# The opening of a mixed attention and feed-forward kernel: value row 0 loaded whole ahead of x, x turned by whole transposes between the first value products

## The chip, the cores and the metric

The kernel runs on one core of a Trainium2 chip. Its time is the device time of one execution in microseconds. The core has a matrix engine (PE, with its weight loads shown apart as PEld), a vector engine (DVE), a scalar engine (ACT), a general engine (POOL) and a sync engine (SP), which here only issues transfers. Each takes its instructions in the order in which they were written and waits on semaphores. 16 DMA engines carry out the transfers that SP and ACT issue.

## The reference

```python
x = A_x                                          # [1, 2048, 640] bf16
g = sigmoid((x * gate_w).sum(-1, keepdims=True))
q, k, v = split(x @ wqkv)                        # 32 heads of 20
phi(u) = concat(softmax(u @ w_phi), softmax(-(u @ w_phi)))   # per head
a = (phi(q) @ (phi(k).T @ v)) / (phi(q) @ sum(phi(k)) + 1e-6) @ wo
b = (gelu(x @ w_gate) * (x @ w_up)) @ w_down     # 640 -> 1728 -> 640
out = g * a + (1 - g) * b
```

All inputs and the output are bf16. The matrix products need x with its 640 features on the partitions, so x has to be turned; the kernel holds it as `xT`, five blocks of 128 features by 2048 tokens.

## The kernel before, in words

Tokens are worked in 16 tiles of 128. The kernel runs in stages: the values, keys and queries of all tiles with the state of the linear attention, then the feed-forward part with the attention's numerators between, then the down projections with the output. The order of all instructions is written out by hand; a small helper, `_Sched`, records for each tile or PSUM bank (a key such as `("ps", 2)`) who wrote and read it last, and adds the waits that follow from that.

The change lies in the first 12 us, in `loads` and in the head of `attention_state`. Only tiles 0 to 3 are concerned. Tiles 4 and up are turned by transposing transfers (`xturn`, L236).

*Transfers.* SP issues, in order: x tiles 0 and 1 (`xload("sp", 0)`), x tiles 2 and 3, the value columns of `wqkv` row block by row block (L249 to L251; row 0 in two pieces, columns 0 to 255 and 256 to 639, keys `("wv", 0)` and `"wv0"`), three chunks of `w_up`, then the transposing transfers of x tiles 4 and 5 and of the key columns `wkT`, and more. ACT issues two small ones: `w_phi` (L276; it waits for POOL's second mask) and the gate vector into `gz` (L279).

*Turning x.* PE first runs dummy products on constants (L675): six of 512 columns, three of 128. `x_transpose(t, ek)` turns a tile by ten transposes of 64 tokens by 128 features, against a 64x64 identity, in two row groups that go to two PSUM banks each, banks (0,1), (4,5), (2,3), (6,7) for tiles 0, 1, 2, 3. One copy per tile takes them to `xT`: DVE for tiles 0 and 2, ACT for tile 1, and half each for tile 3. Six more dummies stand between tiles 1 and 2.

*Values.* `v_step(t, kt)` multiplies feature block `kt` of tile `t` with row block `kt` of the value weights: 480 columns into bank `t`, 160 into bank 4 or 5. A tile needs five such steps. Block 0 is done in two parts per tile (0: the first 256 columns, 1: the others), tiles 0 and 1 first; then blocks 1, 2 and 3 for all tiles.

*Behind it.* `blockdiag` (DVE, L361) spreads `w_phi` with the masks into block-diagonal matrices, in five products. `gate_column(6)` transposes `gz` on PE into bank 6 (L370), and DVE copies it into the weights (L372). Then come block 4 of the four tiles with the copies of the values (ACT and DVE by turns, L493 and L495), three up projections of the feed-forward part (`up_ahead`, L464, into banks 7, 6 and 4), the values of tiles 4 and 5, and the folding of `w_phi` into the key weights (L404), which needs the block-diagonal matrices and `wkT`.

Of the kernel before, what the change touches and what calls it, by code (L numbers as in the profile page):

```python
# [3 lines left out]
P = 128  # L4
BF16 = mybir.dt.bfloat16
F32 = mybir.dt.float32
AF = mybir.ActivationFunctionType
# [100 lines left out]
class _Kernel:  # L108
    S, D, H, DH, F = 2048, 640, 32, 20, 1728
    KD = D // P  # L110
# [111 lines left out]
    def loads(self):  # L222
        sc, nc = self.sc, self.nc
        D, KD, DH, P_ = self.D, self.KD, self.DH, P
        w3 = self.wqkv.rearrange("(kt p) n -> p kt n", p=P)
# [3 lines left out]
        def xload(q, j):  # L229
            sc.dma(q, lambda e: e.dma_start(self.xtok[:, j:j + 2, :], x4[:, j:j + 2, :]),  # L230
                   writes=[("xtok", j), ("xtok", j + 1)])
# [4 lines left out]
        def xturn(t, n):  # L236
# [5 lines left out]
              writes=["gtmp"])  # L242
# [1 line left out]
        sc.op("pool", lambda e: e.affine_select(self.ident[:, :], self.ident[:, :], pattern=[[-1, P]],  # L244
                                                compare_op=ALU.not_equal, fill=1.0, base=0, channel_multiplier=1),
              writes=["ident"])
        xload("sp", 0)
        xload("sp", 2)
        for kt in range(KD):  # L249
            for a, z, key in ((0, self.VA, ("wv", 0)), (self.VA, D, "wv0")) if kt == 0 else ((0, D, ("wv", kt)),):  # L250
                sc.dma("sp", lambda e: e.dma_start(self.w3[:, kt, a:z], w3[:, kt, 2 * D + a:2 * D + z]), writes=[key])  # L251
        u3 = self.wu.rearrange("(kt p) n -> p kt n", p=P)
        a, z = self.UP[0] * P, 7 * P
        sc.dma("sp", lambda e: e.dma_start(self.wu_sb[:, :, a:z], u3[:, :, a:z]), writes=["wue"])
# [4 lines left out]
               writes=["wul"])  # L259
# [5 lines left out]
        for i in range(KD):  # L265
            n = self.HHI[i] - self.HLO[i] + 1
# [6 lines left out]
            pool(lambda e, m=m, n=n, base=base: e.affine_select(  # L273
                m, m, pattern=[[DH, n]], compare_op=ALU.is_ge, fill=0.0, base=DH - 1 - base, channel_multiplier=-1),
                [("mask", i)])
        sc.dma("act", lambda e: e.dma_start(  # L276
            self.wphi_sb[:, :, :], self.wphi.rearrange("h d f -> (h d) f").rearrange("(i p) f -> p i f", p=P)),
            reads=[("mask", 1)], writes=["wphi"])
        sc.dma("act", lambda e: e.dma_start(self.gz[0:KD, :], self.gw.rearrange("(k p) -> k p", p=P)), writes=["gz"])  # L279
        for r in (0, 1):  # L280
            m = self.hmask[:, r, :]
            pool(lambda e, m=m: e.memset(m, 1.0), [("hmask", r)])
# [47 lines left out]
            self.load(self.wd_sb[64 * r:64 * r + 64, 13, :], self.wd[13 * P:self.F, :], ("wd13", r))  # L330
        self.load(self.wo_sb[:, :, :], self.wo.rearrange("(kt p) n -> p kt n", p=P), "wo")

    def x_transpose(self, t, ek):

        sc = self.sc
        b, w = (0, 4, 2, 6)[t], self.D // 2
        bks = (b, b + 1)
        pv = self.bank(b, 1024).bitcast(BF16).rearrange("p (r c) -> p r c", r=2)[:, :, 0:w]
        for c in range(self.KD):
            for r in (0, 1):  # L340
                a = 64 * r
                sc.op("pe", lambda e: e.transpose(
                    pv[:, r, c * 64:(c + 1) * 64], self.xtok[a:a + 64, t, c * P:(c + 1) * P],
                    self.ident[a:a + 64, a:a + 64]),
                    reads=[("xtok", t), "ident"], writes=[("ps", bks[r])], signal=(c == self.KD - 1))
        out = self.xT[:, :, t * P:(t + 1) * P].rearrange("p c (r t) -> p c r t", t=64)
        src = pv.rearrange("p r (c t) -> p c r t", t=64)
        rd = [("ps", b) for b in bks]
        if ek == "ad":
            sc.op("act", lambda e: e.activation(out[:, :, 0, :], src[:, :, 0, :], AF.Copy), reads=rd[:1], writes=[("xh", t)])  # L350
            sc.op("dve", lambda e: e.tensor_copy(out[:, :, 1, :], src[:, :, 1, :]), reads=rd[1:], writes=[("xT", t)])
        elif ek == "a":
            sc.op("act", lambda e: e.activation(out, src, AF.Copy), reads=rd, writes=[("xT", t)])
        else:
            sc.op("dve", lambda e: e.tensor_copy(out, src), reads=rd, writes=[("xT", t)])

    def blockdiag(self):
        DH = self.DH
# [111 lines left out]
            self.mm(bank, bcol, n, self.xT[:, kt, t * P:(t + 1) * P], self.w3[:, kt, c0:c0 + n], kt == 0,  # L470
                    kt == self.KD - 1, [("xT", t)] + [(k, kt) if k != "wgate" else k for k in keys])

    def v_step(self, t, kt, part=None):
        sc = self.sc
        tail = (480, 160, 4 + t // 3, 160 * (t % 3))
        parts = ([(0, self.VA, t, 0)], [(self.VA, 480 - self.VA, t, self.VA), tail], [(0, 480, t, 0), tail])
        for c0, n, bk, col in parts[2 if part is None else part]:
            sc.op("pe", lambda e, c0=c0, n=n, bk=bk, col=col: e.matmul(  # L478
                self.bank(bk)[:, col:col + n], self.xT[:, kt, t * P:(t + 1) * P], self.w3[:, kt, c0:c0 + n],
                start=(kt == 0 and col == 0), stop=(kt == self.KD - 1), skip_group_check=True),  # L480
                reads=[("xT", t), ("xh", t), "wv0" if part == 1 else ("wv", kt)], writes=[("ps", bk)],
                signal=(kt == self.KD - 1))

    def v_first_evac(self, ts, ek, tail):
        sv, nt = ts[0], len(ts)
# [184 lines left out]
    def attention_state(self):  # L670
        NT = self.NT
        sc = self.sc
        ones = self.nc.const_aps.tensor(1.0, [P, 512], BF16)
        for n in (512, 512, 512, 512, 512, 512, 128, 128, 128):
            sc.op("pe", lambda e: e.matmul(self.bank(0, n), ones[:, 0:P], ones[:, 0:n], start=True, stop=True),  # L675
                  writes=[("ps", 0)])
        vs, ve, xt = self.v_step, self.v_first_evac, self.x_transpose
        xt(0, "d")
        xt(1, "a")
        for i in range(3):  # L680
            for a, b in ((0, 2), (64, 3)):
                sc.op("pe", lambda e: e.matmul(self.bank(b, P), ones[a:a + 64, 0:P], ones[a:a + 64, 0:P], start=True,
                                               stop=True), writes=[("ps", b)])
        xt(2, "d")
        xt(3, "ad")
        for t, part in ((0, 0), (1, 0), (0, 1), (1, 1), (2, 0), (2, 1), (3, 0), (3, 1)):
            vs(t, 0, part)
        for kt in range(1, 4):
            for t in range(4):
                vs(t, kt)  # L690
        self.blockdiag()
        self.gate_column(6)
        for t in range(4):
            vs(t, 4)
            ve([t], "ad"[t % 2], False)
            if t == 2:
                ve([0, 1, 2], "a", True)
        ve([3], "d", True)
        v, k, q = self.v_tile, self.k_tile, self.q_tile
        self.up_ahead(0, 7, "d")  # L700
        self.up_ahead(1, 6, "a")
        self.up_ahead(2, 4, "d")
        v(4, 2)
        self.v_split(5, 0)
        m, t, p = "main", "tail", "strip"
        self.fold("k", (3, 4, 6, 5, 7), (0, 1), [(m, 0), (m, 1), (m, 2), (m, 4), (p, 6), (t, 0), (t, 1)])
        v(6, 2)
        v(7, 4)
        k(0, 6)
        self.up_ahead(3, 0, "a")  # L710
        self.up_ahead(4, 2, "a")
        self.k_sums(0)
        self.fold("q", (4, 5, 0, 3, 1), (6, 7), [(m, 0), (m, 1), (p, 4), (m, 2), (m, 4), (p, 0), (t, 0), (t, 1), (p, 5)],
                  2)
        k(1, 2)
        k(2, 4)
        k(3, 0)
        v(8, 2)
        self.strip(1, "a", self.KN)
        self.k_scale(0)  # L720
        for t in range(1, 4):
            self.k_norm(t)
        nk, nv, ng, nq = 4, 9, 0, 0
        self.nq, self.half = 0, 1
        pieces = self.gate_pieces()

        def turn():
            self.half ^= 1
            return (5, 0)[self.half]
        for s in range(NT):  # L730
            r = s % 4
            if r != 1:
                if nk in (4, NT - 1):
                    k(nk, turn())
                else:
                    self.kq_tile(nk, turn())
                self.k_norm(nk)
                nk += 1
            if s and r != 0:
                self.gram(ng)  # L740
                ng += 1
            if s and r in (0, 1):
                v(nv, turn())
                nv += 1
            if s == NT - 1 or r == 1 or s == 0:
                q((0, 4, 1, 2, 3, NT - 1)[nq], turn())
                nq += 1
            if s:
                pieces.pop(0)()
        for p in pieces:  # L750
            p()
        self.down_weights()
# [286 lines left out]
```

## Time and profile before

| | us |
|---|---|
| time, median of three executions | 283.66 (283.25 to 283.87) |
| the profiled execution: span from its first to its last instruction | 282.4 |
| the profiled execution's own time, by the profile | its span; nothing is shown of what lies around it |
| PE busy, of that span | 278.6 |
| PE at work without a break from | 6.19 |
| first up projection starts on PE | 11.53 |
| granted PE clock, mean over the span | 1.00 |

Lines of the timeline have start, duration, engine, line and what is written from what, with the idle time before it and what ended that in brackets. Lines of groups have the busy time of all and the mean of one. Those of transfers have the size and the time from issue to landing. Times are in us from the start of the span, means in ns.

### The profile page before, as it was taken

Reading aid. Unit: us, or ns where it says so; the run is one execution under the profiler, and the core shown is the slowest. Engines: PE = TensorE matmul, PEld = TensorE weight load, DVE = VectorE, ACT = ScalarE, POOL = GpSimd, SP = SyncE. Lnnn points to the kernel's source line nnn. Section 1 sums busy time; section 2 is a strip of 40 time slices with the busy share of each in tenths; the row PEclk is TensorE's granted clock in tenths of the full one; section 3 lists DMA queues with packets and bytes.
Section 4 is the critical chain, followed back from the end, with each engine's and each line's share of the span. In section 5 each row is a group of like instructions: output and inputs, shape, how many; then the busy total and the mean of one; then the engine's idle time right before and its main releaser. Section 6 shows DMA issues by size and latency. Waiting matters only on the chain.

```text
span 282.4 us, 6904 instructions
## 1 busy us (share of the span) xinstructions
PE 278.6 (99%) x2926; PEld 168.6 (60%) x2926; DVE 173.2 (61%) x329; ACT 105.9 (38%) x204; POOL 15.1 (5%) x69
## 2 busy tenths in 40 slices
PE   7999999999999999999999999999999999999996
PEld 4566766665665444444444444445777777777786
DVE  1456999999997523694333324235883883883801
ACT  3246978777793332223232232321112112112011
POOL 7511001101000000000000000000000000000000
PEclk9999999999999999999999999999999999999999
DMA  7999169787789910011000000000133132532221
GB/s 213 193 223 190 29 127 172 153 175 149 157 175 274 350 51 0 2 24 23 2 0 0 0 2 0 0 0 2 26 50 98 46 49 78 66 49 73 73 72 49
DMA packets 60378, 24.11 MB, mean 85 GB/s; under 512 B 51002, under 2 KB 59834, under 8 KB 60346
## 3 DMA queue, kind: packets, MB, share of 16 engines
q1 hardware_dynamic: 59680, 23.63, 38.9%
q8 instruction: 23, 0.38, 0.6%
q10 hardware_dynamic: 666, 0.03, 0.2%
q14 instruction: 9, 0.07, 0.1%
HBM read 9.04 MB, written 2.62 MB: 41 GB/s over the span
## 4 chain that ended last, share of the span: by engine, by line
PE 97%; DMA 1%; SPq 0%; ACT 0%; issue 0%
PE ps L464 58%; PE ps L898 29%; PE ps L599 4%; PE ps L817 2%; PE ps L478 2%; PE ps L637 2%; DMA w<-in_A_wqkv_dram 1%; PE ps L404 1%; SPq L230 0%; SPq L251 0%; ACT outsb L911 0%; PE ps L370 0%
## 5 line engine op out<-in xcount | busy, mean ns | idle before, releaser
L464 PE MATMUL ps<-xT,wu_sb 128*128 128x512 bf16 x260 | 64.1, 379 | 0.0
L464 PE MATMUL ps<-xT,wg_sb 128*128 128x512 bf16 x260 | 63.9, 379 | 0.0
L779 ACT ACTIVATE gl<-ps 128x512 bf16<-128x512 f32 x52 | 31.0, 597 | 70.3 <-PE ps L464 70.3
L464 PE MATMUL ps<-w,xT 128*128 128x362 bf16 (+5 forms) x340 | 51.4, 302 | 0.0
L898 PE MATMUL ps<-wd_sb,hT 64*128 64x320 bf16 x648 | 48.4, 296 | 0.0
L781 DVE TENSOR_TENSOR hT<-ps,gl 128x512 bf16<-128x512 f32 x34 | 23.4, 689 | 37.7 <-PE ps L464 37.7
L464 PEld LDWEIGHTS ps<-xT,wu_sb 128*128 128x128 bf16 x260 | 25.4, 98 | 30.3 <-DVE hT L781 0.2
L464 PEld LDWEIGHTS ps<-xT,wg_sb 128*128 128x128 bf16 x260 | 25.1, 98 | 29.8 <-issue 0.2
L911 ACT ACTIVATE outsb<-ps,Gm 128x320 bf16<-128x320 f32 (+2 forms) x31 | 14.5, 515 | 71.8 <-PE ps L898 71.8
L464 PEld LDWEIGHTS ps<-w,xT 128*128 128x128 bf16 x340 | 31.9, 97 | 14.8
L898 PEld LDWEIGHTS ps<-wd_sb,hT 64*128 64x128 bf16 x648 | 30.9, 94 | 12.2 <-issue 0.4
L898 PE MATMUL ps<-wo_sb,goT 64*128 64x320 bf16 (+2 forms) x340 | 26.5, 288 | 0.0
L617 DVE TENSOR_REDUCE Dk<-Ek 128x66 f32<-128x1320 bf16 x16 | 24.3, 1520 | 2.3 <-ACT gcol L528 2.3
L626 DVE TENSOR_TENSOR Ek<-Ek,Dk 128x1320 bf16<-128x1320 bf16 x16 | 24.5, 1532 | 0.5
L863 DVE TENSOR_TENSOR O<-ps,RH 128x640 bf16<-128x640 f32 x32 | 24.7, 815 | 0.0
L538 ACT ACTIVATE Ek<-ps 128x627 bf16<-128x627 f32 x32 | 20.5, 693 | 6.4 <-PE ps L599 4.9
L538 ACT ACTIVATE Eqt<-ps 128x627 bf16<-128x627 f32 x32 | 20.6, 705 | 2.5 <-PE ps L464 2.5
L781 DVE TENSOR_TENSOR xT<-ps,gl 128x512 bf16<-128x512 f32 x13 | 9.0, 690 | 18.2 <-PE ps L464 18.2
L898 PEld LDWEIGHTS ps<-wo_sb,goT 64*128 64x128 bf16 x340 | 15.9, 94 | 5.3
L898 PE MATMUL ps<-wd_sb,xT 64*128 64x320 bf16 (+2 forms) x270 | 16.0, 269 | 0.0
L851 DVE RECIPROCAL RH<-ps 128x32 f32<-128x32 f32 x16 | 5.7, 357 | 14.4 <-PE ps L817 14.3
L898 PEld LDWEIGHTS ps<-wd_sb,xT 64*128 64x128 bf16 x270 | 12.1, 94 | 2.7
(90 smaller groups left out, 184.1 us busy)
## 6 DMA issues: line engine op xcount, KB each, us to landing
out_dram<-outsb SPq DMA_DIRECT2D x7, 320.0 KB, 2.3
wd_sb<-in_B_w_down_dram SPq DMA_DIRECT2D x1, 2080.0 KB, 11.0
wg_sb<-in_B_w_gate_dram SPq DMA_DIRECT2D x5, 224.0 KB, 3.1
wg_sb<-in_B_w_gate_dram SPq DMA_DIRECT2D x5, 192.0 KB, 3.5
wu_sb<-in_B_w_up_dram SPq DMA_DIRECT2D x5, 192.0 KB, 3.9
wo_sb<-in_A_wo_dram SPq DMA_DIRECT2D x1, 800.0 KB, 9.7
xtok<-in_A_x_dram SPq DMA_DIRECT2D x2, 320.0 KB, 3.3
w<-in_A_wqkv_dram SPq DMA_DIRECT2D x4, 160.0 KB, 4.0
```

The source lines that it names most:

```text
L464: self.sc.op("pe", lambda e: e.matmul(self.ps[:, bank * 512 + c0:bank * 512 + c0 + n], lhs, rhs, start=first, stop=fin), reads=reads, writ ...
L478: sc.op("pe", lambda e, c0=c0, n=n, bk=bk, col=col: e.matmul(self.bank(bk)[:, col:col + n], self.xT[:, kt, t * P:(t + 1) * P], self.w3[:, ...
L538: self.sc.op("act", lambda e: e.activation(dst, src, AF.Exp, scale=scale), reads=[("ps", b), ("ps", b + 1)], writes=[(name, sl, s)])
L599: self.sc.op("pe", lambda e: e.matmul(out, self.xT[:, kt, t * P:(t + 1) * P], self.w3[:, kt, c:c + 2 * n].rearrange("p (r w) -> p r w", w= ...
L617: self.sc.op("dve", lambda e: e.tensor_reduce(self.Dk[:, se, 0, :].rearrange("p (u h) -> p u h", h=self.HG), self.k_view(se), AX.X, ALU.ad ...
L626: sc.op("dve", lambda e: e.tensor_tensor(v, v, R.rearrange("p (u h) -> p u h", h=self.HG).unsqueeze(3).to_broadcast([P, 2 * self.G, self.H ...
L779: sc.op("act", lambda e: e.activation(self.gl[:, slot, :], self.bank(banks[0]), AF.Gelu_apprx_tanh), reads=[("ps", banks[0])], writes=[("g ...
L781: sc.op("dve", lambda e: e.tensor_tensor(hT, up, self.gl[:, slot, :], ALU.mult), reads=[upk, ("gl", slot)], writes=[("hT", hk, c)], guard=old)
L851: dve(lambda e: e.reciprocal(R(0), Dn[1]), rb, [key(0)], guard=old)
L863: dve(lambda e, o=o, f=f, s=s: e.tensor_tensor(o, V[s][:, :, 0:DH], f, ALU.mult), rb + [key(6 + s)], [("O", s, sl)], guard=old)
L898: sc.op("pe", lambda e: e.matmul(self.bank(bk, w), lhs, rhs, start=opens and x == 0, stop=end and not opens, skip_group_check=True), reads ...
L911: sc.op("act", lambda e: e.activation(dst, self.bank(bk, w), AF.Copy, scale=g), reads=rd, writes=wr)
```

## The change

SP issues value row 0 as one transfer, ahead of the two x loads; the other rows follow behind the x loads. The two ACT transfers are taken out of `loads` and put into a function of their own, `small_loads`, that is called behind the last of the four tiles' transposes, without the wait for a mask. The dummies ahead of the transposes are now seven of 512 columns and eight of 128.

`x_transpose(t)` turns a tile by five whole 128x128 transposes: feature blocks 0 to 2 into one bank, copied by DVE, blocks 3 and 4 into the next, copied by ACT. Tiles 0 and 2 use banks 6 and 7, tiles 1 and 3 banks 2 and 3. Tiles 2 and 3 are turned behind the first and second value step. A value step for blocks 0 to 2 waits only for DVE's copy. Three dummies of 128 columns stand behind tile 1.

```diff
-        xload("sp", 0)
-        xload("sp", 2)
         for kt in range(KD):
-            for a, z, key in ((0, self.VA, ("wv", 0)), (self.VA, D, "wv0")) if kt == 0 else ((0, D, ("wv", kt)),):
-                sc.dma("sp", lambda e: e.dma_start(self.w3[:, kt, a:z], w3[:, kt, 2 * D + a:2 * D + z]), writes=[key])
+            sc.dma("sp", lambda e: e.dma_start(self.w3[:, kt, 0:D], w3[:, kt, 2 * D:3 * D]), writes=[("wv", kt)])
+            if kt == 0:
+                xload("sp", 0)
+                xload("sp", 2)
...
-        sc.dma("act", lambda e: e.dma_start(
-            self.wphi_sb[:, :, :], self.wphi.rearrange("h d f -> (h d) f").rearrange("(i p) f -> p i f", p=P)),
-            reads=[("mask", 1)], writes=["wphi"])
-        sc.dma("act", lambda e: e.dma_start(self.gz[0:KD, :], self.gw.rearrange("(k p) -> k p", p=P)), writes=["gz"])
...
+    def x_transpose(self, t):
 
         sc = self.sc
+        b = (6, 2)[t % 2]
+        for ek, bk, c0, c1, key in (("dve", b, 0, 3, "xh"), ("act", b + 1, 3, 5, "xT")):
+            pv = self.bank(bk).bitcast(BF16)[:, 0:(c1 - c0) * P].rearrange("p (c t) -> p c t", t=P)
+            for c in range(c0, c1):
+                sc.op("pe", lambda e: e.transpose(pv[:, c - c0, :], self.xtok[:, t, c * P:(c + 1) * P], self.ident[:, :]),
+                      reads=[("xtok", t), "ident"], writes=[("ps", bk)], signal=c == c1 - 1)
+            out = self.xT[:, c0:c1, t * P:(t + 1) * P]
+            sc.op(ek, lambda e: e.tensor_copy(out, pv) if ek == "dve" else e.activation(out, pv, AF.Copy),
+                  reads=[("ps", bk)], writes=[(key, t)])
+
+    def small_loads(self):
+        sc = self.sc
+        sc.dma("act", lambda e: e.dma_start(
+            self.wphi_sb[:, :, :], self.wphi.rearrange("h d f -> (h d) f").rearrange("(i p) f -> p i f", p=P)),
+            writes=["wphi"])
+        sc.dma("act", lambda e: e.dma_start(self.gz[0:self.KD, :], self.gw.rearrange("(k p) -> k p", p=P)), writes=["gz"])
...
+    def v_step(self, t, kt):
+        for c0, n, bk, col in ((0, 480, t, 0), (480, 160, 4 + t // 3, 160 * (t % 3))):
+            self.sc.op("pe", lambda e: e.matmul(
                 self.bank(bk)[:, col:col + n], self.xT[:, kt, t * P:(t + 1) * P], self.w3[:, kt, c0:c0 + n],
                 start=(kt == 0 and col == 0), stop=(kt == self.KD - 1), skip_group_check=True),
-                reads=[("xT", t), ("xh", t), "wv0" if part == 1 else ("wv", kt)], writes=[("ps", bk)],
-                signal=(kt == self.KD - 1))
+                reads=[("xh" if kt < 3 else "xT", t), ("wv", kt)], writes=[("ps", bk)], signal=(kt == self.KD - 1))
...
-        for n in (512, 512, 512, 512, 512, 512, 128, 128, 128):
+        for n in (512,) * 7 + (128,) * 8:
             sc.op("pe", lambda e: e.matmul(self.bank(0, n), ones[:, 0:P], ones[:, 0:n], start=True, stop=True),
                   writes=[("ps", 0)])
         vs, ve, xt = self.v_step, self.v_first_evac, self.x_transpose
-        xt(0, "d")
-        xt(1, "a")
+        xt(0)
+        xt(1)
         for i in range(3):
-            for a, b in ((0, 2), (64, 3)):
-                sc.op("pe", lambda e: e.matmul(self.bank(b, P), ones[a:a + 64, 0:P], ones[a:a + 64, 0:P], start=True,
-                                               stop=True), writes=[("ps", b)])
-        xt(2, "d")
-        xt(3, "ad")
-        for t, part in ((0, 0), (1, 0), (0, 1), (1, 1), (2, 0), (2, 1), (3, 0), (3, 1)):
-            vs(t, 0, part)
-        for kt in range(1, 4):
+            sc.op("pe", lambda e: e.matmul(self.bank(0, P), ones[:, 0:P], ones[:, 0:P], start=True, stop=True),
+                  writes=[("ps", 0)])
+        vs(0, 0)
+        xt(2)
+        vs(1, 0)
+        xt(3)
+        self.small_loads()
+        for t, kt in ((0, 1), (2, 0), (1, 1), (3, 0), (2, 1), (3, 1)):
+            vs(t, kt)
+        for kt in (2, 3):
             for t in range(4):
                 vs(t, kt)
         self.blockdiag()
         self.gate_column(6)
```

More of the change, by code (lines that the diff above doesn't have):

```diff
@@ L331, in down_weights @@
         self.load(self.wo_sb[:, :, :], self.wo.rearrange("(kt p) n -> p kt n", p=P), "wo")
-    def x_transpose(self, t, ek):
+    def x_transpose(self, t):
         sc = self.sc
[L336 to L355, printed above, removed]
@@ L471, in proj @@
                     kt == self.KD - 1, [("xT", t)] + [(k, kt) if k != "wgate" else k for k in keys])
[L473 to L478, printed above, removed]
+    def v_step(self, t, kt):
+        for c0, n, bk, col in ((0, 480, t, 0), (480, 160, 4 + t // 3, 160 * (t % 3))):
+            self.sc.op("pe", lambda e: e.matmul(
                 self.bank(bk)[:, col:col + n], self.xT[:, kt, t * P:(t + 1) * P], self.w3[:, kt, c0:c0 + n],
                 start=(kt == 0 and col == 0), stop=(kt == self.KD - 1), skip_group_check=True),
-                reads=[("xT", t), ("xh", t), "wv0" if part == 1 else ("wv", kt)], writes=[("ps", bk)],
-                signal=(kt == self.KD - 1))
+                reads=[("xh" if kt < 3 else "xT", t), ("wv", kt)], writes=[("ps", bk)], signal=(kt == self.KD - 1))
     def v_first_evac(self, ts, ek, tail):
```

## The prediction

> **What bounds the kernel now.** I read the page first: busy shares and the chain that ended last.
>
> ```profile
> PE 278.6 (99%) x2926; PEld 168.6 (60%) x2926; DVE 173.2 (61%) x329; ACT 105.9 (38%) x204; POOL 15.1 (5%) x69
> ...
> PE 97%; DMA 1%; SPq 0%; ACT 0%; issue 0%
> ```
>
> PE ends the kernel and is idle for 3.8 us of 282.4. So what counts is the moment from which PE runs without a break, and how much PE work lies behind it. The change touches only the start; the chain of its first 12 us says what ends last there:
>
> ```profile
> 1.73 0.42 SPq L251
> 2.20 3.95 DMA w<-in_A_wqkv_dram
> 6.15 0.05 issue
> 6.19 4.35 PE ps L478 x34
> 10.54 0.06 PE ps L370
> 10.60 1.09 PE ps L478 x8
> ```
>
> The second piece of value row 0 lands at 6.15; from 6.19 on PE has work until the end. The timeline of the same stretch gives the steps:
>
> ```profile
> 0.84 3.04 PE L675 MATMUL ps<-const-bfloat16-1.0 128*128 128x512 bf16 x9 [0.84 <-PEq L1024]
> 3.99 0.47 PE L342 MATMUL ps<-ident,xtok 64*128 64x64 bf16 x20
> 4.29 0.34 PE L682 MATMUL ps<-const-bfloat16-1.0 64*128 64x128 bf16 x6
> 5.37 0.38 PE L478 MATMUL ps<-w,xT 128*128 128x256 bf16 x2
> 10.38 0.22 PE L370 MATMUL ps<-ident,gz 128*128 128x128 bf16 x1
> 10.44 1.25 PE L478 MATMUL ps<-w,xT 128*128 128x480 bf16 x8
> 11.53 3.40 PE L464 MATMUL ps<-xT,wu_sb 128*128 128x512 bf16 x15
> ...
> 2.85 0.43 ACTq L276 DMA_DIRECT2D wphi_sb<-in_A_w_phi_dram  x1
> 3.30 0.67 ACTq L279 DMA_DIRECT2D gz<-in_gate_w_dram  x1
> ...
> 5.05 3.77 SPq L238 DMA_TRANSPOSE xT<-in_A_x_dram  x1
> 8.86 4.78 SPq L234 DMA_TRANSPOSE wkT<-in_A_wqkv_dram  x1
> ```
>
> My yardstick is 11.53, when the first up projection starts: behind it PE never waited for a transfer (the list of waits names DMA only for x and the value rows), so a shift there goes to the end unchanged. Landings and mean durations come from the issue list and the groups by form:
>
> ```profile
> xtok<-in_A_x_dram SPq DMA_DIRECT2D x2, 320.0 KB, 3.3
> wu_sb<-in_B_w_up_dram SPq DMA_DIRECT2D x1, 480.0 KB, 5.7
> wphi_sb<-in_A_w_phi_dram ACTq DMA_DIRECT2D x1, 25.0 KB, 4.5
> ...
> L675 PE MATMUL ps<-const-bfloat16-1.0 128*128 128x128 bf16 x3 | 0.5, 311 | 0.0
> L370 PE MATMUL ps<-ident,gz 128*128 128x128 bf16 x1 | 0.2, 217 | 0.0
> ```
>
> The last two are one shape: 311 ns in the dummies, 217 ns later. PE is slow at the start, and the transposes at 3.99 already run fast (20 in 0.30 us).
>
> **The change part by part.** *Loads.* SP issues every 0.47 us (0.80, 1.27, 1.73, 2.20). One issue in place of two for row 0, now ahead of x: x tiles 0 and 1 are issued 0.47 later, rows 1 to 4 and all behind them 0.47 earlier. x 0 landed 3.1 after its issue (its own row), at 3.9. Low end: the 160 KB vanish in the first transfer's start-up and x is there at 3.99 as now. High end: 1.27 + 3.1 and a little, 4.45. PE takes up the two queued x loads of 320 KB 0.78 apart (3.99 and 4.77), so 160 KB ahead cost about 0.4; I take 4.42 for PE's start on x. Row 1 then lands at 2.20 + 4.0 = 6.2, the later rows by 8.5; below they are needed at 6.4 and later. The row 1 cover is 0.2 us; if it is gone, its lateness adds one for one. Nobody waits for the SP transfers that move 0.47 ahead.
>
> *Dummies.* Seven of 512 at 0.427 (spacing of the weight loads, 2.07 to 2.50) from 0.84 end at 3.8; eight of 128 at 0.055 fast or 0.107 slow end at 4.2 to 4.65. At 4.42 x decides; this is the other bound on the transposes' start: 4.2 to 4.65.
>
> *Transposes and products*, from that start T = 4.42. The gate column, a whole 128x128 transpose, holds PE for 0.06 (10.38 to 10.44); twenty at 0.055 make 1.1 us where forty halves took 0.6, so PE gets 0.5 us more work. A value step (480 + 160 columns) takes 0.274 (four in 1.09). The first DVE copy starts 0.14 after the last of its three transposes ends (as now on ACT: 4.46 to 4.59), takes 0.35 for 384 columns (315 ns for 320, 491 for 640) and is done at T+0.83. PE: tiles 0 and 1 to T+0.56, three dummies to 0.72, wait to 0.88, step (0,0) to 1.15, tile 2 to 1.43, (1,0) to 1.70, tile 3 to 1.98, (0,1) to 2.25. Step (2,0) now writes bank 2, which holds tile 3's transposes until their DVE copy is done: they end at T+2.03, copy from 2.17 to 2.52, so PE waits 0.33, to 2.58. Behind it stand all remaining steps. Thirteen more steps to T+6.14, gate column to 6.20, four steps to 7.30: 11.72 against 11.53, **+0.19**. The earlier wait for row 0 (0.44) is gone, its worth spent on x landing later, 0.5 of transposes and two small waits. Bounds: T alone gives -0.2 to +0.25, bank 2's wait 0 to 0.5.
>
> *w_phi and the gate row.* Both issues move behind ACT's four x copies. The last of these starts once tile 3's transposes are through, T+2.28 = 6.70, so w_phi goes out at about 6.7 (7.1 if the issue waits for the copy's end), gz 0.45 later, 3.9 us later than now. gz is needed by the gate column, which PE reaches at T+6.14 = 10.56, with four value steps and everything else behind it in order. The trace has no ACT transfer beside transposes. Bounds for the queue of the two: 3.1 (quickest load, x 0) has it landed at 9.8, no wait; 5.7 (wu_sb, the load queued beside the transposes) at 12.4, wait 1.85. I take 4.5, its own row, under a load as heavy (the 16 DMA engines' share was 1.17 from 6.19 to 10.31): landed at 11.2, PE goes on at 11.25, **+0.7**. On DVE the five block-diagonal products (1.18) stand ahead of the gate copy and of the value copies: 12.4, gate copy 12.6, value copies to 14.2. The second up projection takes the gate column's bank at 13.5 and tile 4 takes bank 3 at 15.7, so 0.9 us of cover remains; beyond it lateness would add there, but PE has by then waited as long for gz. w_phi's small packets leave the value rows alone and now fall among tile 4's transposed x, landed at 13.1 and used at 14.8: covered by 1.7.
>
> *Sum:* +0.19 + 0.7 = +0.9 on the span of 282.4, of which the median 283.66 stands 1.26 away (launch and end around the span, left as is): 284.5.
>
> On whether the dummies suffice, a row and a rule differ. Row: the clock was up by 3.99, 3.15 us after PE's first work. The Trainium skill (TensorE: Matmul & The Clock Gate, Part 1: The HAM clock gate) says the clock opens after a busy window of about 3.4 us that runs free of the kernel; read strictly that is 4.25 at the earliest, and up to 3.4 later. By the row the sum stays; by the rule both kernels would start slow in some executions, and the one with fewer breaks gains: the last rival.
>
> **Rivals.**
> *A: gz is in time.* If the two small transfers pass beside stalled transposes as fast as x 0 (3.1), PE never waits there: 283.66 + 0.19 = 283.85. For it: w_phi is only 25 KB, and its row was taken beside four value rows. Against: 640 packets, and PE reaches the gate row 3.9 us after the issue.
> *B: forecast*, 284.5.
> *C: transposes hold it up.* Landing by wu_sb's 5.7: wait 1.85, 285.7. For it: the transposed x took 8.0 us to land. Against: wu_sb has 20 times the bytes.
> *D: ACT's issue has to wait for SP's transposes.* SP issues them from about 4.6 to 8.4 and 8.4 to 13.2 without a gap. If ACT gets in only at 8.4, both land near 12.9: wait 2.3, 286.2; if gz falls behind the second, 290 or more. Against: ACT's issue at 2.85 ran 0.43 beside SP's at 2.67, neither longer than alone; no row shows it beside a transpose. The Trainium skill (Perfetto Trace Analysis, DMA Instruction — HWDGE) says that an issuing sequencer locks the descriptor generator for itself; no run here shows that with transposes.
> *E: faster, by the clock.* If PE's clock in timed runs of before opens only after its breaks (4.47 to 4.77, 5.6 to 6.19), transposes and first products run at half speed: 0.6 us of transposes and 0.55 of steps doubled, 1.1 lost, which the unbroken dummies to 4.4 save. With gz in time that is 283.85 - 1.1 = 282.8; it decides only if the opening comes after 5.4. Against: the three times differ by only 0.62, and the profile shows 3.99.
> That row 0 wasn't the limit at all is excluded by the chain.
>
> **How the numbers follow.** B 0.42, A 0.30, C 0.12, D 0.08, E 0.08. The measurement tells about 0.2%, 0.57 us. Slower by more: C, D, most of B (0.34) and a little of A (its +0.25 end; 0.02) make 0.56; faster: E and a trace of A, 0.09; the rest, 0.35, within. The forecast 284.5 is B's. The range runs from A's low end (T early, 283.5) to D's mild case, 286.2; outside lie E and D's worse half and some of A. B alone: 284.1 to 285.0.
>
> **What would show it.** In the profile after: x tile 0's transposes at 4.2 to 4.65; a wait of 0.3 before step (2,0) with DVE's copy as releaser; ACT's two issues near 6.7; a PE wait on gz before L370's successor near 10.6 (none: A; near 2 us: C; ACT issues stretched or after 8.4: D); the first up projection at 12.2 to 12.6. I am wrong if PE reaches it by 11.6, or if row 1 or the transposed x becomes what PE waits for.

## The result, and the profile after

| | before | changed |
|---|---|---|
| median, us | 283.46 (283.18 to 283.87, 4 runs) | 286.24 (285.45 to 286.93, 4 runs) |
| ratio, 95% interval | | 1.0095, 1.0073 to 1.0118 |
| span of the profiled execution | 282.4 | 284.6 (its own time 285.83) |
| first up projection starts on PE | 11.53 | about 12.97 |

The change makes the kernel 2.8 us slower, 0.95%. The forecast was 284.5; the time lies 0.04 above the upper end of the range, 286.2. (In the profile after, the first of the 15 products of the up projection has no record; the second starts at 13.18 and they are 0.215 apart. Other starts of the up projection below are worked out in the same way where the first record is missing.) The ratios leave out two executions, both at 289.6 and both of the experiment with shorter dummies, in which the granted clock was 0.994.

The timeline of the changed kernel, PE first, then ACT's and SP's issues (columns as before):

```profile
0.83 4.00 PE L663 MATMUL ps<-const-bfloat16-1.0 128*128 128x512 bf16 x15 [0.83 <-PEq L1014]
4.63 1.12 PE L336 MATMUL ps<-ident,xtok 128*128 128x128 bf16 x10
...
5.75 0.43 PE L467 MATMUL ps<-w,xT 128*128 128x480 bf16 x2
6.02 0.44 PE L336 MATMUL ps<-ident,xtok 128*128 128x128 bf16 x5
...
7.45 3.72 PE L467 MATMUL ps<-w,xT 128*128 128x480 bf16 x26 [0.16 <-DVE xT L339]
...
11.80 0.23 PE L362 MATMUL ps<-ident,gz 128*128 128x128 bf16 x1 [0.63 <-DMA gz<-in_gate_w_dram]
...
13.18 3.18 PE L456 MATMUL ps<-xT,wu_sb 128*128 128x512 bf16 x14
...
7.06 0.43 ACTq L344 DMA_DIRECT2D wphi_sb<-in_A_w_phi_dram  x1
7.53 0.86 ACTq L347 DMA_DIRECT2D gz<-in_gate_w_dram  x1
...
4.57 2.57 SPq L238 DMA_TRANSPOSE xT<-in_A_x_dram  x1
7.18 4.83 SPq L234 DMA_TRANSPOSE wkT<-in_A_wqkv_dram  x1
```

Four things are to be seen. The dummies last until the transposes start, at 4.63. The first transposes come 0.107 apart until about 5.4, the later ones 0.056 apart: the first ran at half speed, and the ten of tiles 0 and 1 hold PE for 0.95 us (4.63 to 5.58; the 1.12 of the line counts the last one to its end). PE waits before step (2,0), from 7.13 to 7.45. And PE waits for gz, from about 11.0 to 11.80.

The chain of what ended last now runs through that transfer, issued at 7.53:

```profile
7.53 4.22 DMA gz<-in_gate_w_dram
11.76 0.05 issue
11.80 0.23 PE ps L362
12.03 1.10 PE ps L467 x8
```

Up to the up projection 1.44 us are lost. The span grew by 2.2, so 0.7 more is lost elsewhere, and it is at the very end: from the first up projection to the end of PE's last product both kernels take 268.77. These are the stores as SP issues them, in the last microseconds, before and after (durations are min, median, max of the last two):

```profile
L922 SPq DMA_DIRECT2D out_dram<-outsb x2: 372/372/373, 279.9 to 280.8; - x2
```

```profile
L912 SPq DMA_DIRECT2D out_dram<-outsb x2: 372/724/1075, 281.3 to 282.2; - x2
```

The last store took 1.08 us to issue in place of 0.37. Nothing of this kind was in the prediction. In that stretch (281.3 to 283.0) the DMA queues show the stores (q1) and one transfer that is not a store (q8):

```profile
q1 hardware_dynamic: 258, 0.12, 26.6%
q8 instruction: 1, 0.02, 4.8%
```

It is a 16 KB fetch of instructions; it starts at 281.57, 0.05 after PE's last product started. Before, the last such fetch started at 279.34, 0.74 ahead of the start of PE's last product.

### The profile page after: what moved, and what is told of

Its sections match the earlier page's. It is cut to its first block, busy times and chain, and to the rows that moved or that the text cites. A ratio compares the mean times of both kernels' runs of the same rounds, so it can differ in the third digit from the quotient of the medians.

```text
span 284.6 us, 6845 instructions
## 1 busy us (share of the span) xinstructions
PE 279.2 (98%) x2891; PEld 170.0 (60%) x2905; DVE 173.3 (61%) x330; ACT 106.3 (37%) x206; POOL 15.1 (5%) x69
## 4 chain that ended last, share of the span: by engine, by line
PE 95%; POOL 2%; DMA 1%; issue 1%; ACT 0%; POOLq 0%
PE ps L456 57%; PE ps L888 28%; PE ps L587 4%; PE ps L807 2%; PE ps L625 2%; DMA gz<-in_gate_w_dram 1%; PE ps L396 1%; POOL vaug L288 0%; PE ps L467 0%; POOL mask L270 0%; POOL mask L273 0%; POOL hmask L279 0%; POOL hmask L282 0%; ACT outsb L901 0%; POOL ident L244 0%
## 5 line engine op out<-in xcount | busy, mean ns | idle before, releaser
L456 PE MATMUL ps<-xT,wu_sb 128*128 128x512 bf16 x256 | 63.3, 379 | 0.3
L456 PE MATMUL ps<-xT,wg_sb 128*128 128x512 bf16 x250 | 61.8, 379 | 0.5 <-issue 0.2
```

Source lines behind the costliest of these rows:

```text
L456: self.sc.op("pe", lambda e: e.matmul(self.ps[:, bank * 512 + c0:bank * 512 + c0 + n], lhs, rhs, start=first, stop=fin), reads=reads, writ ...
```

## The experiments

The theory after this profile has three costs: gz comes late since queued transposing transfers hold it; the start is later and slower; and the end meets an instruction fetch. Rivals are named in each expectation. All times are compared with runs of the kernel before on the same chip (medians of 283.09, 283.21 and 283.52).

### The two small transfers early again

```diff
+        self.small_loads()          # in loads(), at the old place, behind the second mask
...
         xt(3)
-        self.small_loads()
```

> The changed kernel with the two small transfers (w_phi, gz) issued where they were before, behind POOL's second mask. The changed kernel took 286.2 (span 284.6 profiled), before 283.5. Theory (three costs: gz late 0.8; later start and slow clock in the transposes 0.6 at least; an instruction fetch beside the last store 0.7): PE no longer waits for gz, the first up projection moves from 12.97 to about 12.2, the end about 0.8 earlier, 285.4. Rival (the gate wait only covers another lateness, of value rows now slowed by w_phi's packets, or of DVE): a new wait on a value row or on DVE takes its place and the time stays at 286.0 to 286.4.

Measured: 284.66, ratio 1.0049 (1.0031 to 1.0068). PE goes through the gate column without a wait:

```profile
10.63 0.22 PE L363 MATMUL ps<-ident,gz 128*128 128x128 bf16 x1
10.69 1.26 PE L468 MATMUL ps<-w,xT 128*128 128x480 bf16 x8
11.78 3.40 PE L457 MATMUL ps<-xT,wu_sb 128*128 128x512 bf16 x15
```

The placement of the two transfers is worth 1.6 of the 2.8 us by the medians, more than the 0.8 expected, and 1.2 up to the up projection in these two profiles. In this one the clock also came up earlier (transposes 0.72 for ten), so not all of that is gz. No wait on a value row or on DVE took its place; a short one for x tiles 2 and 3 (0.16, ahead of the transposes at 5.63) is new. The last store's issue was 0.91 here too.

### The two small transfers late, alone

```diff
         xt(3, "ad")
+        sc.dma("act", ... wphi_sb ...)      # taken out of loads(), without the mask's wait
+        sc.dma("act", ... gz ...)
```

> The kernel before with this part of the change alone: w_phi and gz issued by ACT behind its x copies, so at about 5.3 in place of 2.85. Theory 'transposes hold the two transfers': their packets start only when the transposed x of tiles 4 and 5, issued at 5.05, is through (some 11), gz lands at 12 or later, PE waits 1.5 to 2.5 at the gate column and the time is 285.0 to 286.0. Rival 'they just take 4.5 to 4.7 from issue, whatever runs beside': gz lands at about 10.0, before PE reaches the gate column at 10.4, no wait, and the time is that of before or up to 0.3 better (value rows no longer beside 640 small packets): 283.2 to 283.5.

Measured: 287.71, ratio 1.0145 (1.0105 to 1.0185), by the medians worse than the whole change. The four executions differ: 288.63 (the profiled one) and 288.53 with a mean granted clock of 0.994, 286.88 and 286.31 with 1.00, so 2.8 us and more are lost without the lower clock too. The two go out at 5.2 and 5.7, and PE waits for gz until 13.47:

```profile
5.19 0.47 ACTq L682 DMA_DIRECT2D wphi_sb<-in_A_w_phi_dram  x1
5.70 0.94 ACTq L685 DMA_DIRECT2D gz<-in_gate_w_dram  x1
...
13.47 0.23 PE L366 MATMUL ps<-ident,gz 128*128 128x128 bf16 x1 [3.49 <-DMA gz<-in_gate_w_dram]
```

gz lands 7.7 us after its issue. The rival (4.5 to 4.7 whatever runs beside) is out. The wait is longer than expected, and it has two parts. The packets of ACT's queue start at 8.6 and pass among those of the transposes until 11.2. PE is released 2.2 us after the last of them: the DMA queues of the stretch 11.7 to 13.0 show 31 packets in all, on SP's queue, where the stretches of the same length around it have 815 to 1480:

```profile
q1 hardware_dynamic: 31, 0.01, 5.7%
```

What stopped the packets and the landing there is not shown. Behind the wait PE's granted clock is down to half for 3.4 us (stretches, with the busy times of PE, PEld, DVE, ACT and POOL, then the clock):

```profile
13.47:14.03 0.56, 0.56 (x5) 0.35 (x6) 0.56 (x4) 0.09 (x1) 0.00 (x0) 1.00 1.28 291
14.03:17.44 3.41, 3.41 (x12) 1.54 (x11) 1.94 (x6) 1.52 (x3) 0.00 (x0) 0.50 1.11 216
17.44:18.20 0.76, 0.76 (x5) 0.33 (x4) 0.63 (x1) 0.00 (x0) 0.00 (x0) 1.00 0.96 176
```

The Trainium skill (TensorE: Matmul & The Clock Gate, Part 1: The HAM clock gate) says that an idle window of about 3.4 us brings the clock down to half; this trace agrees, with a wait of 3.5.

### Transposes only when the two have landed

```diff
-        xturn(4, 2)
-        wload(self.wkT, D, "wkT")
...
         self.small_loads()
+        self.later()     # SP: xturn(4, 2) waiting for wphi and gz, then wkT and all that followed
```

> The changed kernel, but SP issues the transposing transfers (x tiles 4 and 5, wkT and what follows) only when w_phi and gz have landed; all earlier loads are as they were. Theory 'queued transposes hold the two small transfers': w_phi's packets start 1 to 2 us after the issue in place of 3.0 and gz lands 2 to 3 us after its own issue in place of 4.2, near 10.2, so PE does not wait at the gate column; it waits later instead, for tile 4, whose x comes 2 us or more later. Rival 'w_phi's 640 packets and ACT's late issue make the 4.2': gz lands as late as now, 11.6 or later, and PE waits 0.6 or more at the gate column.

Measured, one execution: 286.36. w_phi lands 2.2 after its issue (at 9.65), where the changed kernel had 4.5, and PE passes the gate column without a wait at 11.43. All packets of ACT's queue (q10) fall between 8.5 and 9.4, the first 1.1 us after the issue (the DMA queues in the stretch 8.5 to 9.4):

```profile
q10 hardware_dynamic: 666, 0.03, 50.3%
```

The list of DMA issues of the stretch 7.5 to 8.5 gives w_phi's time from issue to landing as its last number:

```profile
wphi_sb<-in_A_w_phi_dram ACTq DMA_DIRECT2D x1, 25.0 KB, 2.2
```

In the changed kernel the same queue shows no packet until 10.03 and then 651 of its 666 in 0.6 us (window 10.0 to 10.6), just when the packets of the transposed x, issued at 4.57, end:

```profile
q10 hardware_dynamic: 651, 0.03, 74.3%
q1 hardware_dynamic: 376, 0.09, 67.5%
```

Nor were the DMA engines full meanwhile: from 8.5 to 9.2, again in the changed kernel, SP's queue was the only one with packets and kept the 16 engines busy for 23%:

```profile
q1 hardware_dynamic: 92, 0.04, 22.8%
```

So it was not the 640 packets that took long, nor ACT's issue, nor a want of free engines; the packets stood behind transposes that SP had issued earlier on a queue of its own. The time did not fall, since the transposes are late now: PE waits 1.2 us for wkT at the folding (a later wait was expected, but for tile 4). Together with the experiment before, this shows that the transposes cause gz's lateness. Which part of the transfer path holds the packets is not shown.

### As many PE instructions as before

```diff
         self.blockdiag()
+        for i in range(21):
+            sc.op("pe", ... matmul(self.bank(7, 64), ones[:, 0:P], ones[:, 0:64]) ...)
         self.gate_column(6)
```

> The changed kernel with 21 more dummy products of 64 columns on PE just ahead of the gate column, where PE waits for gz anyway (about 0.6 of 0.8 us): as many PE instructions as the change took away. Theory 'an instruction fetch fell beside the last store' (16 KB at 281.57, last store's issue 1.08 in place of 0.37): the first up projection stays at 12.97, the fetch moves ahead of the end as before, the last store's issue is 0.37 again and the time falls by about 0.7 to 285.5. Rival 'the longer end is chance or has another cause': the end stays 3.0 behind the last product and the time stays at 286.2.

Measured: 285.37 (285.17 to 285.65), ratio 1.0070 (1.0053 to 1.0087), 0.9 less than the change. The first up projection stays at 13.00, the stores take 0.37 each, and the last fetch starts at 280.83, 0.72 ahead of the start of PE's last product. That is as expected, but the next experiment shows that the same can come without the added products.

### The changed kernel, a second profile

> The changed kernel, a second profile. If gz's wait and the fetch at the last store belong to the kernel and not to one execution: PE waits 0.5 to 1.0 at the gate column, gz lands 4 or more after its issue, and the last store's issue takes 0.7 or more; time 285.4 to 287. If they were chance, one of them is missing.

Measured: 284.93. gz comes 3.9 after its issue, at 11.56, and PE waits for it, 0.4 by the distance of the products. The last store's issue is 0.37 here, and no fetch starts after 275.6. The wait, the store and the time are all below what was expected. So gz's wait belongs to the kernel, and the long store doesn't come in each execution: it was seen in the two profiles (the change, and the small transfers early) whose last fetch started 0.05 to 0.08 after PE's last product had started, and in none of the others. The fetch is thus suspected as its cause, and that is not settled: in the kernel before, a store issued at 279.89 beside a fetch (279.34 to 280.41) took 0.37. Nor is it shown that the 21 products moved the fetch, since it also moved between two executions of one kernel.

### The load order alone

```diff
-        xload("sp", 0)
-        xload("sp", 2)
         for kt in range(KD):
-            ...
+            sc.dma("sp", ... whole row kt ..., writes=[("wv", kt)] + (["wv0"] if kt == 0 else []))
+            if kt == 0:
+                xload("sp", 0)
+                xload("sp", 2)
```

> The kernel before with the load order alone changed: value row 0 whole, ahead of the two x loads. x tiles 2 and 3 landed at 4.5 to 4.7 in the three profiles with x first, and at 5.5 to 6.4 in the seven with row 0 first. Theory 'whichever of the first 800 KB goes last lands at 5.5 to 6.4, and it is worse when that is x': x 0 lands at 4.25, x 2 at 5.5 to 6.4, PE turns tiles 2 and 3 then and starts the values 0.4 later, first up projection at 11.6 to 12.4 (before 11.53), time 283.6 to 284.3. Rival 'row 0 first is paid back, since PE no longer waits for its second piece': values start as early as before, first up projection at 11.2 to 11.5, time 283.2 to 283.4 or less.

Measured: 284.54 (284.22 to 285.99), ratio 1.0063 (1.0039 to 1.0088). The profiled execution is the slowest of the five, 285.99. In it x tiles 2 and 3 land at 6.3, and PE waits for them with the turning and all of the values behind:

```profile
4.10 0.72 PE L343 MATMUL ps<-ident,xtok 64*128 64x64 bf16 x20 [0.22 <-DMA xtok<-in_A_x_dram]
...
6.35 0.72 PE L343 MATMUL ps<-ident,xtok 64*128 64x64 bf16 x20 [1.22 <-DMA xtok<-in_A_x_dram]
...
7.00 5.83 PE L479 MATMUL ps<-w,xT 128*128 128x256 bf16 x36
```

The 36 products of the last line take 5.83; in the second profile of the kernel before (shown below) the same 36 take 4.63; the clock was still down when the wait was over, until 9.6. The loss is 1.45 us by the medians, more than expected, so the rival is out. Times from issue to landing of the two x loads (min, median, max), kernel before, changed, this one:

```profile
DMA to landing us min/median/max: 3.1/3.3/3.5
```

```profile
DMA to landing us min/median/max: 3.0/3.6/4.2
```

```profile
DMA to landing us min/median/max: 2.8/3.7/4.6
```

The maximum is that of tiles 2 and 3. With x first (five profiles) it is 3.2 to 3.5 after an issue at 1.27, so they land at 4.5 to 4.7; with row 0 first (nine profiles) 3.7 to 4.7 after 1.73, so 5.4 to 6.4. The second piece of row 0, the last of the same 800 KB before, landed at 5.3 to 6.2. In either order the last of these bytes lands there; before it was three fifths of one row block, now it is half of x.

### The longer dummies alone, and the kernel before again

```diff
-        for n in (512, 512, 512, 512, 512, 512, 128, 128, 128):
+        for n in (512,) * 7 + (128,) * 8:
```

> The kernel before with the changed dummies alone (seven of 512, eight of 128 columns). In the profiles with the dummies of before, PE's clock was up at the first transposes, by 3.8 to 4.3; with the longer ones it came up at 4.05, 4.4, 4.9, 5.4, 6.3 and 6.6. Theory 'chance of the execution, not the dummies': the clock comes up anywhere between 3.6 and 6.7; transposes start at 4.2 to 4.65 and the values at 6.2 as before, since they wait for the second piece of row 0; time 283.2 to 283.6. Rival 'longer dummies delay the clock': it comes up after 4.4, the transposes and first products run slow, time 283.8 to 284.5.

Measured: 283.97, ratio 1.0023 (1.0011 to 1.0035). The clock came up at 4.45, the transposes started at 4.68 and ran fast, the values started at 5.69. The cost, 0.9 us by the medians over 283.09 and 0.65 by the ratio, is of the rival's size, but in this profile not by its mechanism: the dummies hold the transposes back, and row 0's second piece, landed at 5.3 here, no longer covers it.

> The kernel before, a second profile. If the clock's opening is chance, it may come up as late as 6.7 here; if it goes with the shorter dummies, it is up by 4.3 again. First up projection at 11.0 to 11.6, last store's issue 0.37, time 283.0 to 283.9.

Measured: 283.13. This profile shows a late clock with the shorter dummies too:

```profile
3.86 0.72 PE L342 MATMUL ps<-ident,xtok 64*128 64x64 bf16 x20
...
4.70 0.73 PE L342 MATMUL ps<-ident,xtok 64*128 64x64 bf16 x20
...
5.36 4.63 PE L478 MATMUL ps<-w,xT 128*128 128x256 bf16 x36
```

The half transposes take 0.72 for twenty, not 0.47: here the kernel before, too, turned x at half speed, until after 5.1, and still had its first up projection at 10.98: the transposes and the first two value products were through when row 0's second piece landed, at 5.6. The clock comes up by the execution, between 3.6 and 6.7 in these profiles and later where PE waited (the load order alone). Whether longer dummies make a late clock more frequent stays open: it was up by 4.3 in four of six profiles with the shorter ones and in one of eight with the longer ones. That row 0 landed at 5.6 and not at 6.15 made this one of the quicker executions; the profile that the prediction used was one of the slower.

### Shorter dummies in the changed kernel

```diff
-        for n in (512,) * 7 + (128,) * 8:
+        for n in (512,) * 6 + (128,) * 3:
```

> The changed kernel with the dummies of before (six of 512 and three of 128 columns, over at 3.9). Theory 'the dummies, not x, held up the transposes': x landed near 4.3, so the transposes start at 4.35 in place of 4.63; at the slow clock they take as long as now, gz is issued as much earlier, so everything up to the up projection moves by 0.25 and the time by about 0.25, to 286.0 (the end may shift by up to 0.7 either way with the place of the instruction fetch, which the profile shows). Rival 'the longer dummies open the clock': the clock then opens later than 5.4 by up to some us, more steps run slow, and the time grows by 0.3 to 1.5.

Measured: 285.40 (seven executions, 284.59 to 289.65), ratio 1.0075 (1.0040 to 1.0110). In the profile (285.23) the transposes start at 4.33, as expected, and run fast, but then PE waits for x tiles 2 and 3 until 6.45 (0.88 shown), so the first up projection starts at 13.06, no earlier. The arrival of x decides here, not the dummies. The last store's issue is 0.37, so the time can't be set against that of the changed kernel's first profile. No trace shows where the executions above 288 lost their time.

### What is left without gz and with the end as before

```diff
-        for n in (512,) * 7 + (128,) * 8:       # and the small transfers early
+        for n in (512,) * 7 + (32,) * 29:
```

> The changed kernel with w_phi and gz issued where they were (alone: 284.7, first up projection at 11.78, last store's issue 0.91) and with the eight dummies of 128 columns cut into 29 of 32, the same PE time at the slow clock but 21 products more, so that the instruction fetch near the end falls earlier. Theory 'what is left after gz is the start, +0.25, and the fetch, about 0.7': last store's issue 0.37 again, the first up projection stays within 0.3 of 11.8, time 283.6 to 284.0. Rival 'something else keeps the changed kernel slow': the time stays at 284.5 or more with the store's issue at 0.37.

Measured: 284.62, ratio 1.0045 (1.0031 to 1.0058); the store's issue is 0.37, but the first up projection starts at 12.45: tiles 2 and 3 landed at 6.3 and PE waited for them. The expectation failed: what is left is not 0.25 but some 1.4 us. In the profile, the wait for x is 0.55 of it (from 5.76 to 6.30).

```diff
+        sc.dma("act", ... gz ...)               # in loads(); w_phi stays behind the x copies
...
-        self.blockdiag()
         self.gate_column(6)
...
         self.up_ahead(0, 7, "d")
+        self.blockdiag()                        # and the 29 short dummies
```

> The changed kernel with gz alone issued early (by ACT in the loads), w_phi left behind the x copies, the block-diagonal products moved on DVE behind the copy of the first up projection, and the 29 short dummies of 32 columns. Theory 'the five packets of gz are what PE waits for, w_phi has time': no wait at the gate column, block-diagonal products at 13 to 15, ahead of the folding at 17.8; first up projection at 11.6 to 11.9 and the time 283.5 to 284.0, no better than with both early. Rival 'w_phi's packets among the value rows cost the start 0.3 to 0.5': first up projection at 11.3 or earlier and the time 283.2 or less. Second rival 'w_phi lands too late for the folding': a wait at the folding near 17.8.

Measured: 284.76, ratio 1.0051 (1.0038 to 1.0065). No wait for gz and none at the folding, so five early packets are all that PE needs. But the first up projection is at 12.69, with the clock up only at 6.6, and the time is some 0.8 above what was expected, 1.55 over the kernel before. What is left of the change does not pay for the later start.

```diff
+        sc.dma("act", ... gz ...)               # kernel before: gz early, w_phi behind the x copies,
         self.up_ahead(0, 7, "d")                # blockdiag moved as above
+        self.blockdiag()
```

> The kernel before with gz issued early (without the wait for the mask), w_phi by ACT behind the x copies, and the block-diagonal products on DVE behind the copy of the first up projection. Theory: with w_phi late the value rows come sooner (with both late PE reached the gate column at 9.84, before at 10.31) and with gz early the gate column does not wait: first up projection at 11.0 to 11.2 in place of 11.53, time about 283.0 to 283.2, 0.15% better than before. Rival 'the earlier gate column was chance': first up projection at 11.5 and the time that of before, 283.5. Second rival 'w_phi comes too late': it lands at 13.2 or later, the folding waits and the time is 284 or more.

Measured: 283.42 against 283.21, ratio 1.0007 (0.9998 to 1.0016). The first up projection came at 10.88, a little ahead of what the theory said, but in the second profile of the kernel before it came at 10.98: there is no gain, and the first profile was no measure of it.

## Why the prediction was right or wrong, point by point

*Direction and place: right.* The kernel is slower, through a new PE wait on gz at the gate column. The step "+0.7" measured 0.8 in the first profile (0.6 shown as waited) and about 0.4 in the second.

*Landing by w_phi's own row of 4.5: right in number, wrong in mechanism.* w_phi took 4.5 again. But unhindered it takes 2.2 (transposes held back), and the row came from beside other loads. So the number was luck. The mechanism is that of rival C, transposes hold it up: PE passes the gate column early when they are held back, and in the kernel before with late small transfers gz took 7.7, beyond C's 5.7. C's chance of 0.12 was too low, and its price, taken from a plain load, was no upper end. Rival D did not happen: ACT issued at 7.06 in 0.43, and in the kernel before with late small transfers in 0.47 at 5.19, in the midst of a transposing issue of SP (5.05 to 8.33).

*Start of the transposes, 4.42, bounds 4.2 to 4.65:* 4.63, at the upper end, and for the reason named there: eight dummies at the slow clock. x 0 landed at 4.3, so x did not decide.

*Transposes at 0.055: mis-sized.* They came 0.107 apart until about 5.4, and the ten of tiles 0 and 1 held PE for 0.95 in place of 0.56. The clock was read from one profile, as up by 3.99. The rule that the prediction set against this row, a window that runs free of the kernel (Trainium skill, TensorE: Matmul & The Clock Gate, Part 1: The HAM clock gate), was the better guide: the opening lies between 3.6 and 6.7 over the profiles. The earliest opening that the prediction worked out from it, 4.25, did not hold: in the first profile the clock was up by 3.99. Rival E drew the wrong conclusion: in the one profile with a late clock the kernel before loses next to nothing by it, since it needs row 0 at 5.6 anyway; the change has put that cover away.

*Tiles 2 and 3 of x: the step that failed.* The prediction gave 0.4 as the price of the 160 KB ahead, worked it out for tile 0 alone and had no wait for tiles 2 and 3. They land at 5.90 and 5.75 in the two profiles of the changed kernel, where the kernel before had 4.73 and 4.65, so 1.1 to 1.2 later. Two loads behind each other at 0.78 were taken as a price per byte; but the last of the first 800 KB lands at 5.3 or later in either order, and the 0.44 wait for row 0 was counted as gone while the same lateness moved to x. In these two profiles the slow transposes hid this (tile 2 is turned at 6.02 and 6.19), so it shows there as a cover that quicker transposes could not have used; in five of the experiments with row 0 first PE waited for it, up to 1.2 us.

*Wait for bank 2, 0.33:* 0.32 to 0.33 between the products in the profiles of the changed kernel and of its variants. Right.

*The end:* not foreseen. In the first profile the last store cost 0.7; in the second it cost nothing.

*The sum.* By its own terms the first up projection comes at 12.41. In the profiled execution it came at 12.97: step (2,0) started 0.45 late (0.21 from the start of the transposes, the rest from their slow clock), and the wait for gz was 0.1 longer. With the 0.7 at the end, that is the whole distance between 284.5 and this execution's 285.83. In the second it came at 12.77 with no loss at the end, and the time was 284.93. No profile shows the 0.4 from 285.83 to the median of 286.24. In the difference to the kernel before, 0.8 forecast and 2.8 measured, another 0.2 is the base: 283.66 was the median of three executions, 283.46 that of four.

## What to carry to other kernels

In this kernel a small transfer that PE needs soon has to be issued ahead of transposing transfers, even if these go out on another queue; its size said nothing of its landing. When loads are put in another order, ask what now lands last and who needs it: the bytes ahead of it are the same, and a wait that disappears in one place comes back where the last load is used. A step that hides beneath a wait (here the slow clock beneath the wait for row 0) shows its price only when the wait is gone, and one profile of the start is not enough to price either.

## What the runs showed of the hardware that was not expected

- In the changed kernel packets of ACT's queue started 3.0 us after the issue, when those of a transpose issued earlier by SP ended, and then 651 of 666 passed in 0.6 us; with the transposes held back they started 1.1 us after the issue. In the kernel before with late small transfers the last of them was through at 11.2, and PE was released only at 13.4.
- The granted clock that the profile gives for a stretch does not show the slow start: in the changed kernel it reads 1.00 from 4.63 to 5.38, while the transposes come 0.107 apart. Spacing and durations show it. Behind the 3.5 us wait in the kernel with late small transfers it did show the lower clock, as 0.50 from 14.03 to 17.44.
- Where a 16 KB instruction fetch falls near the end changed between two executions of the same kernel (the last at 281.57, or at 275.52), and the last store's issue was 0.9 to 1.1 us in the two profiles where that fetch started just behind the start of PE's last product.
